# Attention, SoLU and a second network on one core: layer norm's transposes to the top of a block's first tile, the scores' softmax behind h's maximum, weight conversions up to the last tile

## The chip, the cores and the metric

The kernel runs on one core of a Trainium2 chip. The core has five engines that run side by side and wait for one another by semaphores: TensorE (PE: matrix multiplications; its weight loads are shown as PEld), VectorE (DVE), ScalarE (ACT), GpSimd (POOL) and SyncE (SP), which here issues nearly all transfers. Each engine works through its own queue in the order in which the program issues to it, so an instruction that waits holds up everything behind it on its engine. The metric is the time of one execution on the device in microseconds.

## What is computed

Batch 8, 8 heads, 576 positions, head size 64; 4608 tokens of width 512. Attention works in chunks of 64 positions. Its output passes through two networks:

```python
scores = 1/sqrt(64) * (q_chunk @ k_chunk.T);  attn = softmax(scores);  x = attn @ v_chunk
h  = x @ w_in                      # 512 -> 1024
solu = h * softmax(h)              # over the 1024
ln = (solu - mean) / sqrt(var + 1e-6) * g_ln
y  = ln @ w_out                    # 1024 -> 512
h2 = y @ w_in2                     # 512 -> 2048
out = leaky_relu(h2, 0.01) @ w_out2   # 2048 -> 512
```

The weights arrive as 64-bit floats and are converted on the core.

## The kernel before

**Precision.** Every large product is made of three: each operand is split into a high part (ScalarE copies it, rounding) and a low part (VectorE or GpSimd subtracts the high part), and high x high, high x low and low x high are summed.

**First half.** The tokens go through in 36 tiles of 128 (T = 36). A loop over t from 1 to 37 is a pipeline written out by hand: in round t, called tile t below, the program issues pieces of several tiles of tokens, and the order of the calls is the order on every engine.

- `qk_mm(t + 3)`, `softmax_a`, `softmax_b`, `pt_mm(t + 1)`, `pt_copy(t + 1)`, `pv_mm(t + 1)` are attention: the scores, their maximum and difference on VectorE and exponential on ScalarE (`softmax_a`), their sums on VectorE and the division on GpSimd (`softmax_b`), the transposes of the probabilities on TensorE (line 397, `pt_ps`), a copy to SBUF, and the product with v. `attend(t)` issues the product with v and the scores of a later tile into one pair of PSUM banks, and then `x_split` (lines 439, 444).
- `ff1_mm(t, 0)` and `ff1_mm(t, 1)` are the two halves of h (line 462, 12 matmuls each). h lives in three PSUM banks, so the second half of a tile's h takes the bank of the first half of the tile before.
- `solu_max` (line 477), `solu_a` (the minimum of two negated maxima, line 481; two exponentials on ScalarE, line 485), `solu_b` (the products on VectorE, line 493, which free h's banks), `solu_c` (sum of squares on ScalarE, line 513, and small factors on GpSimd) and `solu_d` (GpSimd scales the tile `us`, line 523) are SoLU and layer norm of tile t - 1.
- `lnT_mm(t - 2)` transposes the layer norm's result on TensorE (line 537), `lnT_hi` (ScalarE, line 548) and `lnT_lo` (VectorE, line 552) split it. These transposes and y share two PSUM banks.
- `y1_group(b, m)` is a quarter of y for a block b of four tiles (line 564, 24 matmuls); ScalarE copies it out (line 572) and SP stores it to `y_d`. Groups start in tile 5; from then on each tile has one. A tile with g = (t - 5) mod 4 = 0 is the first tile of a block of y: 5, 9, 13 to 33.

**Conversions.** The other weights come in pieces: `take_magnitudes` (ScalarE, line 103), `convert_a` and `convert_b` (four operations on VectorE, lines 110 to 120) and `finish`, which for two pieces together makes a weight block: two differences on GpSimd and two on VectorE (lines 193, 194), copies on ScalarE (196) and low parts on GpSimd (197). The block goes to DRAM by `store_next` in the next tile. The number `pieces` says how many pieces a tile converts: 1, or 2 in the tiles of the table DOUBLE. The first pieces are w_out1 (lines 126, 127, 173), which y needs from tile 5 on.

**Between the halves.** At t = 36 attention's memory is given back, and `y_load` (line 254) and `w_load` (line 294) fill the memory of the second half; `y_sum` (line 267) and `y_split` (lines 272, 273) make its operands at t = 37.

**Second half.** The second network by a scheme of seven products (lines 913, 970, 981) instead of eight. The change doesn't touch it.

Of the kernel before, what the change touches and what calls it, by code (L numbers as in the profile page):

```python
# [43 lines left out]
DOUBLE = (5, 6, 7, 14, 15, 22, 23, 30, 31)  # L44
# [8 lines left out]
def kernel(  # L53
# [254 lines left out]
    with tc.manual_schedule():  # L308

        with ExitStack() as phase:  # L310
# [271 lines left out]
            def attend(t):  # L582

                if AHEAD <= t < T - 3:
                    both = two_banks("xs_ps")
                    pv_mm(t + 1, both)
                    qk_mm(t + 3, both)
                    x_split(t + 1)
                    softmax_a(t + 3)
                else:  # L590
                    pv_mm(t + 1)
                    x_split(t + 1)
# [159 lines left out]
            for t in range(1, T + 2):  # L752
                if t == T:
                    att.close()
                    yp = ctx.enter_context(
                        tc.tile_pool(name="yp", bufs=1, side="right", reuse_waits="tile")
                    )
                    ws = ctx.enter_context(
                        tc.tile_pool(name="ws", bufs=WS, side="right", reuse_waits="tile")
                    )  # L760
                    for n in range(4):
                        y_load(0, n)
                    for _ in range(WS):
                        w_load()
# [13 lines left out]
                late = g == 0 or t == T - 1  # L778
                pieces = 0 if t < AHEAD or t >= T - 2 else 2 if t in DOUBLE else 1
# [4 lines left out]
                if 1 <= t <= T:  # L784
                    if t < 3:
                        solu_max(t - 1, 0)
                    solu_max(t - 1, 1)
                    solu_a(t - 1)
                if t <= AHEAD:
                    softmax_a(t + 2)  # L790
                if t > AHEAD and not late:
                    take_magnitudes(pieces)
                if 1 < t < T:
                    ff1_mm(t, 0)
                if 1 <= t <= T:
                    solu_b(t - 1)
# [4 lines left out]
                if t <= AHEAD or (late and t < T - 1):  # L801
                    pt_copy(t + 1)
                if late and t >= 2:
                    lnT_mm(t - 2)
                    lnT_split(t - 2, 0)
                    lnT_split(t - 2, 1)
                if t > AHEAD:
                    if late:
                        take_magnitudes(pieces)
                    convert_a(pieces)  # L810
                    convert_b(pieces)
                if AHEAD < t < T - 1 and not late:
# [8 lines left out]
                if 1 <= t <= T:  # L821
# [10 lines left out]
                if groups and not late:  # L832
# [4 lines left out]
                    if t >= 2:  # L837
                        lnT_mm(t - 2)
                        lnT_split(t - 2, 0)
                        lnT_split(t - 2, 1)  # L840
# [3 lines left out]
                else:  # L844
                    if t >= 2 and not late:
# [7 lines left out]
                    elif t < T - 1 and not late:  # L853
                        attend(t)
                    if 1 < t < T:
                        ff1_mm(t, 1)
                    if late and 1 < t < T - 1:
                        attend(t)
                    if t <= AHEAD:
                        if 2 <= t < AHEAD:  # L860
                            for hf in range(2):
                                lnT_lo(t - 2, hf)
                        finish()
                        take_magnitudes(pieces if t == AHEAD else t < 3)
                        convert_a(pieces if t == AHEAD else t == 3)
                        if t == AHEAD:
                            convert_b(pieces)
                    if t >= AHEAD:
                        finish(pieces)
                    for bm in groups:  # L870
                        y1_group(*bm)

# [295 lines left out]
```

## Time and profile before

| | |
|---|---|
| median of three runs | 1253.04 us (1252.58 to 1253.45) |
| the profiled execution: time, span | 1254.23 us, 1252.4 us |
| mean granted clock of TensorE, share of full speed | 0.993 |
| busy share: TensorE, its weight loads | 97%, 86% |
| busy share: VectorE, ScalarE, GpSimd | 71%, 46%, 23% |
| chain that ended last: TensorE, VectorE, ScalarE | 78%, 14%, 3% |

The span runs from the first to the last instruction; the time of an execution is some 2 us more. An engine's busy share is a mean over both halves: VectorE is busier in the first. The chain that ended last is followed back from the last instruction, at each step to what released it, so its shares say whose work or lateness stands in the time.

### The profile page before, as it was taken

The page shows a single profiled execution, that of the slowest core. Times are in us where ns is not written, and L with a number is a line of the kernel's source. Part 1 is how long each engine was busy: PE and PEld are TensorE (multiplying, and loading weights), DVE is VectorE, ACT ScalarE, POOL GpSimd, SP SyncE. Part 2 cuts the span into 40 slices and gives each one's busy share as a digit, 9 for nine tenths or more (in the row PEclk, how much of TensorE's full clock was granted, in tenths as well). Part 3 has the DMA queues.
Part 4 walks back from the last instruction along what each step waited for, and adds up shares of the span by engine and source line. Part 5 has one row for each costly group of instructions (what it writes and reads, how often), then busy time and mean ns, then how long its engine had stood idle before and what let it go on. Part 6 is the DMA issues. An engine that isn't in the chain of part 4 may idle for free.

```text
span 1252.4 us, 22880 instructions
## 1 busy us (share of the span) xinstructions
PE 1214.1 (97%) x8554; PEld 1074.5 (86%) x8554; DVE 895.5 (71%) x1536; ACT 573.1 (46%) x1079; POOL 284.1 (23%) x388
## 2 busy tenths in 40 slices
PE   4999999899999999999999999999999999999998
PEld 3777887787878777899889988998999899889987
DVE  7778878888887886535785677577666766775674
ACT  6655555555555554423443452344345333442451
POOL 0265656655765665100000000000000000000000
PEclk8899999999999999999999999999999999999999
DMA  7435456645756563469889878988998899789676
GB/s 249 142 111 175 153 184 211 237 160 168 239 184 194 191 194 130 143 214 316 270 284 318 281 242 274 324 256 253 297 307 246 261 303 298 240 264 296 195 224 197
DMA packets 153789, 288.83 MB, mean 231 GB/s; under 512 B 14288, under 2 KB 63440, under 8 KB 152656
## 3 DMA queue, kind: packets, MB, share of 16 engines
q1 hardware_dynamic: 153312, 286.78, 71.0%
q8 instruction: 69, 1.13, 0.4%
q10 hardware_dynamic: 368, 0.59, 0.1%
q14 instruction: 40, 0.33, 0.1%
HBM read 239.08 MB, written 48.23 MB: 229 GB/s over the span
## 4 chain that ended last, share of the span: by engine, by line
PE 78%; DVE 14%; ACT 3%; DMA 2%; issue 1%; POOL 1%; SPq 0%; ACTq 0%; POOLq 0%
PE h_ps L913 28%; PE o_ps L970 19%; PE y_ps L564 11%; PE o_ps L981 10%; PE h_ps L462 7%; DVE us L493 2%; DVE lnT L552 1%; DVE wf L116 1%; DVE wf L120 1%; DVE z L477 1%; DVE es L374 1%; DVE xs L444 1%; PE xs_ps L423 1%; DVE wf L110 1%; DVE st L373 1%
## 5 line engine op out<-in xcount | busy, mean ns | idle before, releaser
L913 PE MATMUL h_ps<-yo,w_s 128*128 128x384 f32 x2016 | 351.1, 335 | 0.0
L913 PEld LDWEIGHTS h_ps<-yo,w_s 128*128 128x128 f32 x2016 | 349.3, 188 | 0.7
L970 PE MATMUL o_ps<-wo_s,yo 128*128 128x512 f32 (+1 forms) x1016 | 262.9, 393 | 0.0
L462 PE MATMUL h_ps<-wi,xs 128*128 128x512 f32 x864 | 214.6, 402 | 12.0 <-DVE us L493 8.4
L564 PE MATMUL y_ps<-lnT,wo 128*128 128x512 f32 (+1 forms) x888 | 206.2, 388 | 4.6 <-DVE lnT L552 2.0
L970 PEld LDWEIGHTS o_ps<-wo_s,yo 128*128 128x128 f32 x1016 | 179.2, 188 | 28.6
L462 PEld LDWEIGHTS h_ps<-wi,xs 128*128 128x128 f32 x864 | 162.3, 192 | 48.0 <-DVE us L493 9.8
L564 PEld LDWEIGHTS y_ps<-lnT,wo 128*128 128x128 f32 x888 | 160.9, 188 | 38.8 <-POOL wo L127 3.2
L981 PEld LDWEIGHTS o_ps<-wo_s,yo 128*128 128x128 f32 x1008 | 144.7, 188 | 15.6
L273 DVE TENSOR_TENSOR yo<-c,yo 128x768 fp32r<-128x768 f32 x144 | 132.6, 954 | 31.9 <-ACT yo L272 31.9
L981 PE MATMUL o_ps<-wo_s,yo 128*128 128x256 f32 x1008 | 149.8, 283 | 0.0
L892 ACT ACTIVATE c<-h_c 128x384 f32<-128x384 f32 x144 | 72.8, 526 | 127.4 <-DVE h_c L924 127.4
L924 DVE TENSOR_TENSOR h_u<-h_ps,h_p 128x384 f32<-128x384 f32 x96 | 53.3, 555 | 106.7 <-PE h_ps L913 100.0
L272 ACT ACTIVATE yo<-c 128x768 fp32r<-128x768 f32 x144 | 113.0, 836 | 7.1 <-DVE c L954 5.5
L493 DVE SCALAR_TENSOR_TENSOR us<-h_ps,us 128x512 f32<-128x512 f32 x72 | 48.6, 691 | 32.7 <-ACT us L485 32.7
L552 DVE TENSOR_TENSOR lnT<-ln_ps,lnT 128x512 fp32r<-128x512 f32 x72 | 45.8, 680 | 33.8 <-ACT lnT L548 33.8
L387 POOL TENSOR_TENSOR es<-es,st 128x512 f32<-128x512 f32 x33 | 34.6, 1047 | 152.4 <-DVE st L386 96.8
L485 ACT ACTIVATE us<-h_ps,z 128x512 f32<-128x512 f32 x72 | 48.6, 681 | 34.3 <-DVE z L481 34.3
L272 ACT ACTIVATE yo<-a 128x768 fp32r<-128x768 f32 x36 | 29.9, 839 | 72.6 <-DVE a L267 72.6
L924 DVE TENSOR_TENSOR h_c<-h_ps,h_u 128x384 f32<-128x384 f32 x96 | 53.2, 554 | 12.8 <-PE h_ps L913 12.2
L380 ACT ACTIVATE es<-es 128x512 f32<-128x512 f32 x33 | 20.9, 632 | 86.7 <-DVE es L374 86.7
L892 ACT ACTIVATE c<-h_ps 128x384 f32<-128x384 f32 x48 | 23.6, 492 | 76.2 <-PE h_ps L913 76.2
(94 smaller groups left out, 1399.0 us busy)
## 6 DMA issues: line engine op xcount, KB each, us to landing
w_s<-wi_d SPq DMA_DIRECT2D x336, 256.0 KB, 4.0
wo_s<-wo_d SPq DMA_DIRECT2D x168, 512.0 KB, 4.6
wi_d<-wi SPq DMA_DIRECT2D x8, 1792.0 KB, 6.4
wo_d<-wi SPq DMA_DIRECT2D x8, 1792.0 KB, 7.2
raw<-in_w_out SPq DMA_DIRECT2D x24, 512.0 KB, 5.6
raw<-in_w_in SPq DMA_DIRECT2D x23, 512.0 KB, 5.3
vs<-in_v SPq DMA_DIRECT2D x144, 64.0 KB, 4.4
a<-y_d SPq DMA_DIRECT2D x24, 384.0 KB, 5.1
```

What stands on the lines that cost most here:

```text
L272: act.activation(o[:, 0], x, AF.Copy)
L273: dve.tensor_tensor(o[:, 1], x, o[:, 0].bitcast(F32), op=ALU.subtract)
L462: pe.matmul(hs[t, n], lhsT=x[:, a, kk, :], rhs=w[:, b, kk % 2, n, :], start=(kk == 0 and a == 0 and b == 0), stop=(kk == KD - 1 and a == 1),)
L485: act.activation(u[:, c], hs[t, n], AF.Exp, bias=z[:, 0:1], accum_out=z[:, 8 + n : 9 + n])
L493: dve.scalar_tensor_tensor(u[:, c], hs.pop((t, n)), 1.0 / FF1, u[:, c], op0=ALU.mult, op1=ALU.mult, accum_out=z[:, 10 + n : 11 + n],)
L552: dve.tensor_tensor(dst[:, 1], ps, dst[:, 0].bitcast(F32), op=ALU.subtract)
L564: pe.matmul(ps[:, part], lhsT=w[:, a, kk % 4, m * P : (m + 1) * P], rhs=lnT[:, c, kk, pairs, :][:, part], start=(kk == 0 and a == 0 and c ...
L892: act.activation(blocks[block, j // 2][:, j % 2], src, AF.Prelu, alpha=0.01)
L913: pe.matmul(ps, lhsT=w[:, a, kk * P : (kk + 1) * P], rhs=y[:, c, kk, :], start=(first and kk == 0 and a == 0 and c == 0), stop=(kk == 1 an ...
L924: dve.tensor_tensor(o, ps, x, op=ALU.add)
L970: pe.matmul(ps[:, : 2 * P * (a.stop - a.start)], lhsT=x[:, 0, kk, m * P : (m + 1) * P], rhs=w[:, kk, a].rearrange("p a n -> p (a n)"), sta ...
L981: pe.matmul(sums[p % 2][m][:, : 2 * P], lhsT=x[:, 1, kk, m * P : (m + 1) * P], rhs=w[:, kk, 0], start=False, stop=(i == PAIRS - 1 and kk = ...
```

## The change

Four things move; no arithmetic is added or removed.

1. In a block's first tile from 9 on (`late`), layer norm's transposes and their high parts go to the top of the tile, ahead of h's maximum, and y's group goes from the end of the tile to the middle, ahead of `attend`. Tile 35 is no longer such a tile.
2. `softmax_a` leaves `attend`. It comes at the top of the next tile, behind h's maximum and `solu_a`.
3. DOUBLE loses 30 and 31, and single conversions go on in tiles 34 and 35 instead. The last store is issued at t = 36 ahead of the loads of y.
4. Tile 5's two conversions start behind the probabilities' copy and end ahead of `solu_c`, not behind `attend`.

The diff, cut to these:

```diff
-DOUBLE = (5, 6, 7, 14, 15, 22, 23, 30, 31)
+DOUBLE = (5, 6, 7, 14, 15, 22, 23)
...
                     both = two_banks("xs_ps")
                     pv_mm(t + 1, both)
                     qk_mm(t + 3, both)
-                    x_split(t + 1)
-                    softmax_a(t + 3)
                 else:
                     pv_mm(t + 1)
-                    x_split(t + 1)
+                x_split(t + 1)
...
                 if t == T:
+                    store_next()
                     att.close()
...
-                late = g == 0 or t == T - 1
-                pieces = 0 if t < AHEAD or t >= T - 2 else 2 if t in DOUBLE else 1
+                late = g == 0 and t > AHEAD
+                pieces = 0 if t < AHEAD or t >= T else 2 if t in DOUBLE else 1
...
-                if 1 <= t <= T:
+                if late:
+                    lnT_mm(t - 2)
+                    for hf in range(2):
+                        lnT_hi(t - 2, hf)
+                if t <= T:
                     if t < 3:
                         solu_max(t - 1, 0)
                     solu_max(t - 1, 1)
                     solu_a(t - 1)
-                if t <= AHEAD:
+                if late:
+                    for hf in range(2):
+                        lnT_lo(t - 2, hf)
+                if t + 2 < T:
                     softmax_a(t + 2)
-                if t > AHEAD and not late:
+                if t > AHEAD:
                     take_magnitudes(pieces)
...
-                if t <= AHEAD or (late and t < T - 1):
+                if t <= AHEAD:
                     pt_copy(t + 1)
-                if late and t >= 2:
+                if t == AHEAD:
+                    take_magnitudes(pieces)
                     lnT_mm(t - 2)
-                    lnT_split(t - 2, 0)
-                    lnT_split(t - 2, 1)
+                    for hf in range(2):
+                        lnT_split(t - 2, hf)
                 if t > AHEAD:
-                    if late:
-                        take_magnitudes(pieces)
                     convert_a(pieces)
                     convert_b(pieces)
-                if AHEAD < t < T - 1 and not late:
+                if AHEAD < t < T - 1:
                     pt_copy(t + 1)
...
+                elif t == AHEAD:
+                    convert_a(pieces)
+                    convert_b(pieces)
...
-                if groups and not late:
+                if t > AHEAD and groups:
                     for bm in groups:
                         y1_group(*bm)
                     if t + 1 < T:
                         attend(t)
-                    if t >= 2:
+                    if not late:
                         lnT_mm(t - 2)
-                        lnT_split(t - 2, 0)
-                        lnT_split(t - 2, 1)
+                        for hf in range(2):
+                            lnT_split(t - 2, hf)
                     if t < T:
                         ff1_mm(t, 1)
                     finish(pieces)
```

TensorE at tile 9, the first tile of a block of y, from the end of tile 8 on. Before (`ln_ps` are layer norm's transposes, four rows of `h_ps` are half an h, `pt_ps` the probabilities' transposes, `y_ps` a group of y):

```order
L462 MATMUL h_ps<-wi_172,xs 128x512 x2
L462 MATMUL h_ps<-wi_353,xs 128x512 x2
L397 MATMUL pt_ps<-ident,es 128x128 x4
L537 MATMUL ln_ps<-ident,us 128x128 x8
L462 MATMUL h_ps<-wi_172,xs 128x512 x4
L462 MATMUL h_ps<-wi_353,xs 128x512 x4
L462 MATMUL h_ps<-wi_172,xs 128x512 x2
L462 MATMUL h_ps<-wi_353,xs 128x512 x2
L423 MATMUL xs_ps<-pt,vs_104 64x64 x16
L360 MATMUL xs_ps<-kb_102,qt 64x64 x16
L564 MATMUL y_ps<-lnT,wo_831 128x512 x12
L564 MATMUL y_ps<-lnT,wo_960 128x512 x12
```

The same place after:

```order
L537 MATMUL ln_ps<-ident,us 128x128 x8
L462 MATMUL h_ps<-wi_172,xs 128x512 x4
L462 MATMUL h_ps<-wi_353,xs 128x512 x4
L462 MATMUL h_ps<-wi_172,xs 128x512 x2
L462 MATMUL h_ps<-wi_353,xs 128x512 x2
L397 MATMUL pt_ps<-ident,es 128x128 x4
L564 MATMUL y_ps<-lnT,wo_831 128x512 x12
L564 MATMUL y_ps<-lnT,wo_960 128x512 x12
L423 MATMUL xs_ps<-pt,vs_104 64x64 x16
L360 MATMUL xs_ps<-kb_102,qt 64x64 x16
L462 MATMUL h_ps<-wi_172,xs 128x512 x4
```

Layer norm's transposes went ahead of the first half of h, and y's group stands between the halves of h instead of behind the second.

VectorE from the end of tile 11 into tile 12, an ordinary tile. Before (L373 and L374 are the scores' maximum and difference, L552 layer norm's low parts, L193 and L194 a weight block, L477 h's maximum, L493 the products, L384 the scores' sums):

```order
L444 TENSOR_TENSOR xs<-xs_ps,xs 128x2x2x128
L373 TENSOR_REDUCE st_2766<-xs_ps 128x8
L374 TENSOR_TENSOR es<-xs_ps,st_2766 128x512
L552 TENSOR_TENSOR lnT<-ln_ps,lnT 128x4x128 x2
L193 TENSOR_TENSOR wc<-wf,wc 128x256
L194 TENSOR_TENSOR wc<-wf,wc 128x256
L477 TENSOR_REDUCE z<-h_ps 128x1
L481 TENSOR_TENSOR z<-z 128x1
L493 SCALAR_TENSOR_TENSOR us,z<-h_ps,us 128x512 x2
L502 TENSOR_TENSOR z<-z 128x1
L384 TENSOR_REDUCE st_2766<-es 128x8
```

The same place after:

```order
L444 TENSOR_TENSOR xs<-xs_ps,xs 128x2x2x128
L552 TENSOR_TENSOR lnT<-ln_ps,lnT 128x4x128 x2
L193 TENSOR_TENSOR wc<-wf,wc 128x256
L194 TENSOR_TENSOR wc<-wf,wc 128x256
L477 TENSOR_REDUCE z<-h_ps 128x1
L481 TENSOR_TENSOR z<-z 128x1
L373 TENSOR_REDUCE st_2818<-xs_ps 128x8
L374 TENSOR_TENSOR es<-xs_ps,st_2818 128x512
L493 SCALAR_TENSOR_TENSOR us,z<-h_ps,us 128x512 x2
L502 TENSOR_TENSOR z<-z 128x1
L384 TENSOR_REDUCE st_2818<-es 128x8
```

The scores' maximum and difference went from ahead of layer norm's low parts to between h's maximum and the products.

SP where the halves meet, before (`wo_d` is a weight block's store, `a` the four loads of y: a11, a21, a22, a12; in brackets what a transfer waits for):

```order
L135 DMA wo_d_84<-wi 896x1x512 [waits DMAHW7_49,Pool_49]
L577 DMA y_d_72<-ys 128x256 [waits DMAHW0_49,Activation_49]
L580 DMA y_d_71<-ys 128x256 [waits DMAHW1_49]
L254 DMA a_5911<-y_d_67 128x2x384 [waits DMAHW2_49,DVE_49]
L254 DMA a_5913<-y_d_67 128x2x384 [waits DMAHW3_49]
L254 DMA a_5915<-y_d_67 128x2x384 [waits DMAHW7_49,DMAHW4_49]
```

And after:

```order
L135 DMA wo_d_84<-wi 896x1x512 [waits DMAHW6_49,Pool_49]
L577 DMA y_d_72<-ys 128x256 [waits DMAHW7_49,Activation_49]
L580 DMA y_d_71<-ys 128x256 [waits DMAHW0_49]
L135 DMA wo_d_84<-wi 896x1x512 [waits DMAHW1_49,Pool_49]
L254 DMA a_5911<-y_d_67 128x2x384 [waits DMAHW2_49,DVE_49]
L254 DMA a_5913<-y_d_67 128x2x384 [waits DMAHW3_49]
L254 DMA a_5915<-y_d_67 128x2x384 [waits DMAHW6_49,DMAHW4_49,DMAHW1_49]
```

A second store stands ahead of the loads of y; it waits for GpSimd, and the third load (a22) waits for it to land (DMAHW1).

## Rows read from the trace of the kernel before

**Rows 1.** Timeline of TensorE: start us, length us, line, operation, count [idle before, releaser].

```profile
90.53 0.60 PE L397 MATMUL pt_ps<-ident,es 128*128 128x128 f32 x4
...
93.46 5.29 PE L564 MATMUL y_ps<-lnT,wo 128*128 128x512 f32 x22 [0.83 <-POOL wo L127]
...
134.82 0.60 PE L397 MATMUL pt_ps<-ident,es 128*128 128x128 f32 x4
...
175.47 0.60 PE L397 MATMUL pt_ps<-ident,es 128*128 128x128 f32 x4
...
188.98 0.60 PE L397 MATMUL pt_ps<-ident,es 128*128 128x128 f32 x4
...
191.59 3.02 PE L462 MATMUL h_ps<-wi,xs 128*128 128x512 f32 x12 [1.13 <-DVE us L493]
...
203.97 0.60 PE L397 MATMUL pt_ps<-ident,es 128*128 128x128 f32 x4
...
231.01 0.60 PE L397 MATMUL pt_ps<-ident,es 128*128 128x128 f32 x4
232.23 5.73 PE L564 MATMUL y_ps<-lnT,wo 128*128 128x512 f32 x24 [0.62 <-DVE lnT L552]
...
246.48 0.60 PE L397 MATMUL pt_ps<-ident,es 128*128 128x128 f32 x4
...
262.38 0.60 PE L397 MATMUL pt_ps<-ident,es 128*128 128x128 f32 x4
...
477.88 4.61 PE L462 MATMUL h_ps<-wi,xs 128*128 128x512 f32 x12 [1.68 <-DVE us L493]
...
508.07 11.08 PE L564 MATMUL y_ps<-lnT,wo 128*128 128x512 f32 x48
```

**Rows 2.** One window, TensorE: us, busy us (count), granted clock, DMA share, GB/s.

```profile
479.00:480.00 1.00, 1.00 (x4) 0.50 0.02 8
```

**Rows 3.** Timeline of VectorE, end of tile 11 and tile 12.

```profile
170.42 0.68 DVE L373 TENSOR_REDUCE st<-xs_ps 128x8 f32<-128x512 f32 x1
...
173.07 1.29 DVE L552 TENSOR_TENSOR lnT<-ln_ps,lnT 128x512 fp32r<-128x512 f32 x2 [1.24 <-ACT lnT L548]
174.28 1.42 DVE L193 TENSOR_TENSOR wc<-wf,wc 128x256 f32<-128x256 f32 x1
...
176.49 0.68 DVE L477 TENSOR_REDUCE z<-h_ps 128x1 f32<-128x512 f32 x1
...
178.42 0.69 DVE L493 SCALAR_TENSOR_TENSOR us<-h_ps,us 128x512 f32<-128x512 f32 x1 [1.06 <-ACT us L485]
...
181.60 1.15 DVE L112 TENSOR_SCALAR wf<-wf 128x512 uint32<-128x512 uint32 x1
```

**Rows 4.** Timeline of GpSimd: the scaling of `us` in tiles 12 and 16.

```profile
185.60 1.21 POOL L523 TENSOR_SCALAR us<-us,z 128x1024 f32<-128x1024 f32 x1
...
244.00 1.20 POOL L523 TENSOR_SCALAR us<-us,z 128x1024 f32<-128x1024 f32 x1
```

**Rows 5.** Timeline of VectorE, one conversion in tile 13 and what follows it.

```profile
194.51 0.43 DVE L110 TENSOR_SCALAR wf<-wf 128x512 f32<-128x512 f32 x1
194.97 0.43 DVE L112 TENSOR_SCALAR wf<-wf 128x512 uint32<-128x512 uint32 x1
...
196.80 0.68 DVE L477 TENSOR_REDUCE z<-h_ps 128x1 f32<-128x512 f32 x1
```

**Rows 6.** Timeline of VectorE where the halves meet.

```profile
505.69 1.29 DVE L552 TENSOR_TENSOR lnT<-ln_ps,lnT 128x512 fp32r<-128x512 f32 x2 [0.49 <-ACT lnT L548]
...
523.57 0.95 DVE L267 TENSOR_TENSOR s<-a,a 128x768 f32<-128x768 f32 x1
```

**Rows 7.** DMA issues from 480 to 560 us: count, KB each, median us to landing.

```profile
wo_d<-wi SPq DMA_DIRECT2D x1, 1792.0 KB, 7.1
a<-y_d SPq DMA_DIRECT2D x4, 384.0 KB, 5.2
```

**Rows 8.** Timeline of ScalarE where the halves meet.

```profile
532.63 0.60 ACT L572 ACTIVATE ys<-y_ps 128x512 f32<-128x512 f32 x1 [1.08 <-issue]
```

More of the change, by code (lines that the diff above doesn't have):

```diff
@@ L794 @@
                     ff1_mm(t, 0)
-                if 1 <= t <= T:
+                if t <= T:
                     solu_b(t - 1)
@@ L820 @@
                     owed = 1
-                if 1 <= t <= T:
+                elif t == AHEAD:
+                    convert_a(pieces)
+                    convert_b(pieces)
+                if t <= T:
                     solu_c(t - 1)
@@ L844 @@
                 else:
-                    if t >= 2 and not late:
+                    if t >= 2 and t != AHEAD:
                         lnT_mm(t - 2)
@@ L852 @@
                         ff1_mm(t, 1, (3,))
-                    elif t < T - 1 and not late:
+                    elif t < AHEAD:
                         attend(t)
-                    if 1 < t < T:
+                    if 1 < t:
                         ff1_mm(t, 1)
-                    if late and 1 < t < T - 1:
+                    if t == AHEAD:
                         attend(t)
[L859 to L869, printed above, removed]
+                    if 2 <= t < AHEAD:
+                        for hf in range(2):
+                            lnT_lo(t - 2, hf)
+                    finish()
+                    if t < 3:
+                        take_magnitudes()
+                    elif t == 3:
+                        convert_a()
                     for bm in groups:
```

## The prediction

> **What bounds the kernel now.** I read the page's busy shares first (in the table above: TensorE 97%, VectorE 71%), then TensorE's own timeline, because an engine that is busy for 97% of the span can only give back its gaps. In the second half (matrix multiplications of the second network, from 543 us on) there are none to speak of, and the change does not touch that half; so I looked for gaps between 75 and 543 us. The timeline shows a beat: each tile issues its four transposes of probabilities once, and from one such row to the next an undisturbed tile takes 13.51 us, from 175.47 to 188.98 [rows 1]. Whatever a tile takes above that is loss. The reader should see five kinds:
>
> - Tiles 6 to 8: 90.53 to 134.82 is 44.29 us for three tiles, 3.76 too many; part of it is y's first group, which waits for w_out1 pieces that GpSimd is still splitting (0.83 in one place).
> - Tile 13, first of a block of y: 14.99, so 1.48 too many. Its second half of h waits 1.13 for VectorE to read the previous h out of PSUM (191.59). Tiles 21 and 29 repeat it with 1.50 and 1.47.
> - Tile 16, after two tiles of double conversions: 15.47, 1.96 too many; y waits for layer norm's low parts on VectorE (232.23). Tiles 24 and 32 repeat it (1.95, 1.96).
> - Tile 17, first of a block and just behind: 15.90, 2.39 too many; tile 25 repeats it (2.38).
> - Tile 33: the same wait (1.68), and then its 12 matmuls take 4.61 where those of tile 13 took 3.02 [rows 1]; the granted clock there is 0.50, the 1.2 GHz level [rows 2]. TensorE had been nearly idle before the drop; the like waits of tiles 17 and 25 had none. I put the loss at 2.39 + 1.59 = 3.98.
>
> Sum: 3.76 + 4.45 + 5.87 + 4.77 + 3.98 = 22.8 us. That is all that the touched part could give.
>
> **The change, part by part.** *Transposes first, y in the middle.* In a block's first tile before, y came last, since layer norm's transposes of that very tile had to come ahead of it; so between the first half of h and the second only short work stood (two groups of transposes), while VectorE needed maximum, exponential and product. Now y's group, with probabilities and scores, stands there as in every other tile, some 7 us more. The waits on h of tiles 13, 21, 29, 17, 25 and 33 go: before, the product in tile 12 ended near 179.8, 7 us behind the end of the previous h [rows 3], and the second half of h comes 13.51 less its own 2.75, so 10.8, behind it. No instruction is added; TensorE issues the same ones.
>
> What can be late instead is the transposes: they now stand at the tile's top, and read u, which GpSimd scales in the tile before. In tile 12 of before, that scaling ends at 185.60 + 1.21 = 186.81 [rows 4], while TensorE would want it at about 188.98 less some 2.75 for 12 matmuls, 186.2 [rows 1]. As things stood, 0.6 late; so what the second edit does to that chain decides.
>
> *Scores' softmax behind h's maximum.* Before, VectorE made the scores' maximum and difference ahead of layer norm's low parts: from 170.42 to 171.83, then it sat idle for 1.24 because ScalarE's high parts stood behind the scores' exponential, which stood behind that difference [rows 3]. Only then came the low parts, a weight block's two differences (174.28 to 176.49) and h's maximum at 176.49, though h had been finished around 172.7. Moved behind the maximum, 1.41 of work and 1.24 of idling leave this stretch: maximum 2.65 earlier. The work falls where VectorE waits 1.06 for h's exponentials anyway, at 178.42 [rows 3], so it costs 0.35 there and not 1.41. Net 2.3 earlier for all that follows, the scaling too: ready at about 184.5 for 186.2. I take no wait in tiles 9, 13, 21, 29 and 33. Scores' exponentials come later by about 5 us, but their transposes come a tile later, so that is covered.
>
> In double tiles VectorE has 2.3 us more of conversions (one takes 194.51 to 196.80 [rows 5]), and its lag adds up: in tile 16 of before the scaling ended at 245.20 [rows 4], and TensorE without its waits would have wanted it at about 246.48 - 2.75 - 1.4 = 242.3. It has to come 2.9 earlier. Two double tiles in a row win 2 x 2.3 = 4.6, or less, since part of the idling was lag that the conversions fill. I take no wait in tiles 17 and 25, with bounds of 0 and 2 each, and count 0.4 for the pair. Tiles 16, 24 and 32 lose their wait on the low parts, now 2.65 earlier against 0.62 of wait [rows 1]; in tile 32 the double conversions ahead are gone too.
>
> *Tile 5's conversions* start behind h's maximum instead of behind the attention's work, some 4 us earlier. They then delay the next x's low part, by 4.6 for two; its user comes after y's first group, which takes 5.5 (half of 11.08 for two at 508.07 [rows 1]), so about 1 is to spare. In return tile 6's weights are split earlier, but GpSimd's multiplication by g now stands ahead of layer norm's factors, so only about 1 us earlier. I take 1.0 off tile 6's loss and all 1.6 off tiles 7 and 8, since everything behind has slack: 2.8 of 3.76, bounds 0 and 3.76.
>
> One rule was weighed here. VectorE's shift of a piece took 0.43 in tile 13 and 1.15 in tile 12 [rows 3, 5]; in tile 12 GpSimd multiplied the probabilities at that moment. The Trainium skill, SBUF — State Buffer, section "Who interferes with whom", says that VectorE's two-port forms and GpSimd hold a shared pair of ports alternately, one blocking the other for a whole instruction. By that rule tile 5's conversions, moved under GpSimd's scaling, would lose up to two such 0.7, 1.4 in all, and the sum would be 0.4 smaller past the cover of 1; the trace agrees with the rule. My sum goes without it.
>
> *Conversions up to the last tile.* Two pieces move from tiles 30 and 31 to 34 and 35. In tile 35 one conversion (2.3 us) and h's maximum (0.68) now precede layer norm's low parts, which ran at 505.69 [rows 6] with y starting at 508.07 [rows 1]. VectorE can begin at about 505.1, so the first low part ends at about 508.8 and y waits 0.8: I take 0.9, bounds 0 and 2. Behind it the last weight block is made in tile 36: GpSimd ends it at about 515.5, and SP now issues its store ahead of the loads of y. The third load (a22) waits until that store has landed, since it takes its memory: 7.1 later, then 5.2 for itself [rows 7], so about 528 where the sum that needs it began at 523.57 [rows 6]. The chain of sums and splits ends 4.5 us later, and with it ScalarE's copy of y's second group, 532.63 before with 1.08 of idling [rows 8], about 536.6 then. Its bank is wanted by y's fourth group at about 538.5. Hidden, with 2 us left; were the block 4 us later, it would cost 2.
>
> **Sum.** Gains 2.8 + 4.45 + 5.87 + 4.77 + 3.98 = 21.9; costs 0.9 + 0.4 = 1.3; net -20.6. The profiled execution took 1254.23, 1.19 over the median of the runs, 1253.04; taken off the median this gives **1232.5 us**, and about 1233.6 for a profiled run.
>
> **The rivals.** (1) *The double tiles stay late.* GpSimd's scaling is too late at the top of tiles 17 and 25 by 2 each, and tiles 16 and 24 keep their 1.96: 7.9 lost, about 1240. For it: VectorE is loaded nearly in full there. The Trainium skill, TensorE: Matmul & The Clock Gate, section "What's actually happening", says that an idle array falls back to 1.2 GHz; tile 33 agrees, tiles 17 and 25 do not. If such a wait brings the slow level as in tile 33, 1.6 more, 1242. Chance 17%.
> (2) *The transposes wait in all seven block tops*, because the softmax in front of the product delays the scaling and nothing else gives the time back: 0.6 + 1.4 = 2.0 each, 14 in all, 1246.5. Against it: the 1.24 of idling has one cause, and that leaves. Chance 6%.
> (3) *The end of the stage*: the store is later than I reckon, and y's last group and the first product wait 3 to 6: 1236 to 1239. Chance 10%.
> (4) *Slower than before*: the same wait as in (2), but more than 20.6 / 7 = 2.9 us each, that is, the scaling 2.3 later than in the rows instead of 2.3 earlier; at 4 us each it would be 1260. The exponentials now stand behind layer norm's high parts on ScalarE in these tiles, 1.1 us; that alone is not enough. Chance 3%. No change to within 0.2% (2.5 us, about what a measurement of this kernel can tell from none) would need 18 us of new waits: 2%.
>
> My forecast has the remaining 62%, with 1230 to 1235 of its own. All 22.8 without any cost would be 1230.2; rival (1) ends at 1240. The range 1229.5 to 1240.5 leaves out rival (1) with the slow clock, (2) and (4). Faster 95%, same 2%, slower 3%.
>
> **What the profile of after would show.** Transposes of probabilities 13.5 us apart from tile 9 to 32; no wait of h on u's product in the tiles named; the granted clock at full through tile 33; h's maximum within 1.5 us of the end of h in ordinary tiles; a wait of about 0.9 of y near the end of the first half; the load of a22 landing some 5 us before y's fourth group. Wrong would be: transposes of layer norm that wait for u on GpSimd, or y's last groups waiting for ScalarE's copies.

## The result, and the profile after

The changed kernel took **1233.01 us** (median of 5 runs, 1231.88 to 1233.18) against 1253.24 (5 runs) for the kernel before on the same chip: ratio 0.984, 95% interval [0.982, 0.985]. The prediction was 1232.5. The total is right; what it put the gain down to is not, as the runs below show.

The page of after: TensorE's share rises from 97% to 98% of a shorter span, and VectorE now waits for TensorE where TensorE waited for VectorE. Columns of the last two rows: line, engine, operation, form, count, then busy us, mean ns, and idle us with its releaser.

```profile
span 1230.9 us, 22882 instructions
...
PE 1208.2 (98%) x8554; PEld 1073.7 (87%) x8554; DVE 900.8 (73%) x1536; ACT 573.1 (47%) x1079; POOL 285.9 (23%) x388
...
L477 DVE TENSOR_REDUCE z<-h_ps 128x1 f32<-128x512 f32 x72 | 48.9, 682 | 20.6 <-PE h_ps L462 20.6
...
L552 DVE TENSOR_TENSOR lnT<-ln_ps,lnT 128x512 fp32r<-128x512 f32 x72 | 46.0, 681 | 6.5 <-ACT lnT L548 6.5
```

The page of before has of the same kind:

```profile
L493 DVE SCALAR_TENSOR_TENSOR us<-h_ps,us 128x512 f32<-128x512 f32 x72 | 48.6, 691 | 32.7 <-ACT us L485 32.7
L552 DVE TENSOR_TENSOR lnT<-ln_ps,lnT 128x512 fp32r<-128x512 f32 x72 | 45.8, 680 | 33.8 <-ACT lnT L548 33.8
```

The low parts (line 552) idled 33.8 us for ScalarE's high parts, 8.2 of them in one wait near the end of the first half; now 6.5, 4.8 of them in one wait. That row holds the cause, as will be seen, but its size alone doesn't tell: the products (line 493) idled nearly as long.

TensorE's timeline at tiles 13, 17 and 33 and at the end of the first half, which answers to [rows 1]:

```profile
182.63 1.03 PE L537 MATMUL ln_ps<-ident,us 128*128 128x128 f32 x8
183.42 3.02 PE L462 MATMUL h_ps<-wi,xs 128*128 128x512 f32 x12
186.27 0.60 PE L397 MATMUL pt_ps<-ident,es 128*128 128x128 f32 x4
...
236.77 1.03 PE L537 MATMUL ln_ps<-ident,us 128*128 128x128 f32 x8
...
453.33 1.03 PE L537 MATMUL ln_ps<-ident,us 128*128 128x128 f32 x8
454.12 3.02 PE L462 MATMUL h_ps<-wi,xs 128*128 128x512 f32 x12
...
486.48 11.18 PE L564 MATMUL y_ps<-lnT,wo 128*128 128x512 f32 x48 [0.47 <-DVE lnT L552]
497.50 1.91 PE L537 MATMUL ln_ps<-ident,us 128*128 128x128 f32 x16
499.57 22.38 PE L564 MATMUL y_ps<-lnT,wo 128*128 128x256 f32 x120 [0.15 <-DVE lnT L552]
521.78 3.47 PE L915 MATMUL h_ps<-yo,w_s 128*128 128x384 f32 x19
```

No wait is left at the tops of blocks, and the 12 matmuls behind tile 33's transposes take 3.02; those that waited there before took 4.61. The granted clock is 1.00 from 130 to 520 us, the 2.4 GHz level. The second half starts at 521.78; before, at 543.26. The transposes of probabilities are 13.5 us apart in ordinary tiles, as forecast; at block tops they now stand behind layer norm's, so a tile of 14.43 and one of 12.66 follow each other there. Neither sign of being wrong is seen: no transpose waits for GpSimd, and y's last groups don't wait for copies.

VectorE in tile 12 answers to [rows 3]:

```profile
166.79 1.28 DVE L552 TENSOR_TENSOR lnT<-ln_ps,lnT 128x512 fp32r<-128x512 f32 x2
167.99 1.37 DVE L193 TENSOR_TENSOR wc<-wf,wc 128x256 f32<-128x256 f32 x1
169.39 0.84 DVE L194 TENSOR_TENSOR wc<-wf,wc 128x256 f32<-128x256 f32 x1
170.16 0.68 DVE L477 TENSOR_REDUCE z<-h_ps 128x1 f32<-128x512 f32 x1
...
172.28 0.68 DVE L493 SCALAR_TENSOR_TENSOR us<-h_ps,us 128x512 f32<-128x512 f32 x1
```

Both idle times of [rows 3], 1.24 and 1.06, are gone. h's maximum starts some 1.1 behind the end of h (near 169.1); before, 3.8. GpSimd's scaling answers to [rows 4]; in tile 16:

```profile
234.94 1.20 POOL L523 TENSOR_SCALAR us<-us,z 128x1024 f32<-128x1024 f32 x1
```

It ends at 236.14, 0.63 ahead of the transposes at 236.77; in tile 12 the margin is 2.16 (180.47 to 182.63).

Where the halves meet, y's copies by ScalarE answer to [rows 8]:

```profile
513.61 1.18 ACT L572 ACTIVATE ys<-y_ps 128x512 f32<-128x512 f32 x2 [1.02 <-DMA y_d<-ys]
```

The second of the two starts at about 514.2 (513.61 + 1.18 - 0.60), 27.7 behind y's start at 486.48, against 24.6 before (532.63 - 508.07); the prediction had 28.5 and called it hidden, as it is: the y that runs from 499.57 has no gap, and its fourth group, which wants that bank, begins near 516.5. The sum that needs a22 begins at 505.10, when that load lands, some 11 us ahead of the fourth group; the 5 that the prediction names among its signs doesn't fit its own sum (528 and 538.5).

### The profile page after: what moved, and what is told of

It reads as the page before. It is cut to its first block, busy times and chain, and to the rows that moved or that the text cites. A ratio compares the mean times of both kernels' runs of the same rounds, so it can differ in the third digit from the quotient of the medians.

```text
span 1230.9 us, 22882 instructions
## 1 busy us (share of the span) xinstructions
PE 1208.2 (98%) x8554; PEld 1073.7 (87%) x8554; DVE 900.8 (73%) x1536; ACT 573.1 (47%) x1079; POOL 285.9 (23%) x388
## 3 DMA queue, kind: packets, MB, share of 16 engines
q8 instruction: 69, 1.13, 0.4%
## 4 chain that ended last, share of the span: by engine, by line
PE 93%; DVE 5%; ACT 1%; POOL 1%; issue 0%; DMA 0%; POOLq 0%; ACTq 0%
PE h_ps L915 28%; PE o_ps L972 19%; PE y_ps L564 16%; PE h_ps L462 14%; PE o_ps L983 10%; PE ln_ps L537 2%; PE xs_ps L423 1%; PE pt_ps L397 1%; PE xs_ps L360 1%; DVE wf L116 1%; DVE wf L120 1%; DVE z L477 1%; DVE us L493 1%; DMA raw<-in_w_in 0%; DVE wf L110 0%
## 5 line engine op out<-in xcount | busy, mean ns | idle before, releaser
L972 PEld LDWEIGHTS o_ps<-wo_s,yo 128*128 128x128 f32 x1016 | 179.3, 189 | 28.5
L477 DVE TENSOR_REDUCE z<-h_ps 128x1 f32<-128x512 f32 x72 | 48.9, 682 | 20.6 <-PE h_ps L462 20.6
L572 ACT ACTIVATE ys<-y_ps 128x512 f32<-128x512 f32 x36 | 21.5, 597 | 82.8 <-PE y_ps L564 81.7
L552 DVE TENSOR_TENSOR lnT<-ln_ps,lnT 128x512 fp32r<-128x512 f32 x72 | 46.0, 681 | 6.5 <-ACT lnT L548 6.5
```

The lines of the kernel that those rows point to most:

```text
L477: dve.reduce_max(sol[t][:, 8 + n : 9 + n], hs[t, n], axis=AX, negate=True)
L552: dve.tensor_tensor(dst[:, 1], ps, dst[:, 0].bitcast(F32), op=ALU.subtract)
L972: pe.matmul(ps[:, : 2 * P * (a.stop - a.start)], lhsT=x[:, 0, kk, m * P : (m + 1) * P], rhs=w[:, kk, a].rearrange("p a n -> p (a n)"), sta ...
```

## The experiments

Each median below stands beside runs of the kernel before on the same chip: 1252.35 for the first four runs, 1253.08 for the next four, 1252.02 for the next three, 1253.98 for the last. "The edits" are numbered as under "The change". The theory at the start was the prediction's: edit 1 is worth 13.2 us (tiles 13, 17, 21, 25, 29, 33), edit 2 5.9 (tiles 16, 24, 32), edit 4 2.8, edit 3 about nothing. The rival: the block tops waited because VectorE was late, so edit 2 is worth nearly all.

**All but edit 2.** After, with the softmax back in `attend`:

```diff
                     qk_mm(t + 3, both)
+                    x_split(t + 1)
+                    softmax_a(t + 3)
...
-                if t + 2 < T:
+                if t <= AHEAD:
                     softmax_a(t + 2)
```

> The kernel after, with the scores' softmax back in attend, ahead of layer norm's low parts. Mine: the first edit alone moves waits to the transposes at the tops, because GpSimd's scaling comes too late: about 0.6 us each in tiles 13, 21, 29 and 33, 1 to 3 in tiles 17 and 25, and tiles 16 and 24 keep their 1.96; together 8 to 12, so 1241 to 1245, and the trace names u on GpSimd as the releaser of the transposes. Rival (the edits simply add; the softmax only helps the double tiles): 1237, no wait of a transpose on GpSimd.

Measured: **1266.3** us, ratio 1.011 [1.009, 1.013]: slower than before, which neither my theory nor the rival had. TensorE at the top of tile 13, and three windows, one in its wait and two behind it (us, busy us of PE, PEld, DVE, ACT, POOL with counts, granted clock, DMA share, GB/s):

```profile
181.61 3.01 PE L462 MATMUL h_ps<-wi,xs 128*128 128x512 f32 x12
186.94 1.23 PE L537 MATMUL ln_ps<-ident,us 128*128 128x128 f32 x8 [2.32 <-DVE lnT L552]
187.86 4.61 PE L462 MATMUL h_ps<-wi,xs 128*128 128x512 f32 x12
```

```profile
185.00:186.00 1.00, 0.00 (x0) 0.00 (x0) 0.00 (x0) 1.00 (x3) 0.01 (x1) 1.00 0.99 301
...
188.00:189.00 1.00, 1.00 (x4) 0.81 (x4) 0.92 (x3) 0.99 (x3) 0.00 (x0) 0.50 0.73 243
189.00:190.00 1.00, 1.00 (x4) 0.81 (x3) 1.00 (x2) 1.00 (x4) 0.00 (x0) 0.50 0.57 154
```

The releaser is not GpSimd's scaling, which the prediction watched (it ended at 185.01), but VectorE's low parts of the transposes before: these must be read out of their banks before the next transposes can be written there. All seven block tops wait so, 16.7 us in all (0.95, four times 2.3, twice 3.2), and behind six of them the clock falls to 1.2 GHz. ScalarE and VectorE there:

```profile
184.96 0.63 ACT L380 ACTIVATE es<-es 128x512 f32<-128x512 f32 x1 [3.46 <-DVE es L374]
185.50 1.07 ACT L548 ACTIVATE lnT<-ln_ps 128x512 fp32r<-128x512 f32 x2
```

```profile
184.23 0.69 DVE L374 TENSOR_TENSOR es<-xs_ps,st 128x512 f32<-128x512 f32 x1
186.11 1.29 DVE L552 TENSOR_TENSOR lnT<-ln_ps,lnT 128x512 fp32r<-128x512 f32 x2 [1.18 <-ACT lnT L548]
```

Difference on VectorE, exponential on ScalarE, high parts on ScalarE, low parts on VectorE: four steps one behind the other. That is the row to keep in mind for the last four runs.

**Edit 2 alone.** The kernel before, with `softmax_a` moved as in after and nothing else:

```diff
-                    softmax_a(t + 3)
...
-                if t <= AHEAD:
+                if t + 2 < T:
                     softmax_a(t + 2)
```

> The kernel before, with nothing but the scores' softmax moved behind h's maximum. Mine: tiles 16, 24 and 32 lose their 1.96 each and tiles 17 and 25 some 0.4 each, but in the block tops 13, 17, 21, 25, 29 and 33 the wait of h grows by about 0.5, because the softmax (1.4) stands ahead of the products and only 0.85 of idling takes it up: about 4 us faster than before, 1249, with h's wait at tile 13 grown from 1.13 to about 1.7. Rival (the softmax costs nothing where it stands): 1246.5, h's wait at tile 13 unchanged or gone.

Measured: **1232.3**, ratio 0.984 [0.982, 0.985], as much as all four edits. From 75 us to the second half TensorE waits once, for 0.15; from tile 8 to 32 no tile is over 0.1 longer than 13.52. In tile 13, where y still comes last, VectorE waits for h and TensorE's second half of h follows the transposes at once:

```profile
183.00 0.69 DVE L477 TENSOR_REDUCE z<-h_ps 128x1 f32<-128x512 f32 x1 [1.24 <-PE h_ps L462]
...
185.74 0.69 DVE L493 SCALAR_TENSOR_TENSOR us<-h_ps,us 128x512 f32<-128x512 f32 x1
```

```profile
185.97 1.04 PE L537 MATMUL ln_ps<-ident,us 128*128 128x128 f32 x8
186.76 3.01 PE L462 MATMUL h_ps<-wi,xs 128*128 128x512 f32 x12
```

So the short work between the halves suffices: it was VectorE that came late, not TensorE that had too little to do.

**All but edit 1**: after, with the transposes, y and `attend` of a block's first tile in the places of before.

```diff
-                if late:
+                if t > T:
                     lnT_mm(t - 2)
                     for hf in range(2):
...
+                if late and t < T:
+                    lnT_mm(t - 2)
+                    for hf in range(2):
+                        lnT_split(t - 2, hf)
+                    take_magnitudes(pieces)
...
+                if late and t < T:
+                    ff1_mm(t, 1)
+                    attend(t)
+                    finish(pieces)
+                    for bm in groups:
+                        y1_group(*bm)
```

> The kernel after, with the block tops 9 to 33 as before (layer norm's transposes behind the probabilities', y last); the other edits stay. Mine: h waits for its products in all of tiles 13 to 33 that are block tops, some 2 each, so 10 to 13 slower than after, 1244 to 1246; whether the clock falls to 1.2 GHz at tile 33 is open, and 1.6 hang on it. Rival (the softmax's move alone gives most): within 5 of after, below 1238.

Measured: **1232.4**, ratio 0.984 [0.982, 0.985]. No wait at any block top, the clock full: the prediction's theory is gone.

**All but edit 4**: tile 5's conversions behind `attend` again.

```diff
                 if t == AHEAD:
-                    take_magnitudes(pieces)
...
-                elif t == AHEAD:
-                    convert_a(pieces)
-                    convert_b(pieces)
...
+                    elif t == AHEAD:
+                        take_magnitudes(pieces)
+                        convert_a(pieces)
+                        convert_b(pieces)
+                        finish(pieces)
```

> The kernel after, with tile 5's two conversions back behind the attention's work. Mine: tiles 6 to 8 lose about 2.8 again, 1235.8; y waits for w_out1's low parts on GpSimd in each of the three. Rival (the softmax's move has already taken this loss away): 1233, and only tile 6 waits.

Measured: **1231.8**, ratio 0.983 [0.982, 0.985]; the rival was right that the softmax's move had taken this loss away. Tiles 6 to 8 take 41.74 us together where those of after take 42.09: without edit 4 they are 0.35 shorter, not longer, and the wait of tile 6 for GpSimd's w_out1 pieces is gone.

**All but edit 3**: DOUBLE with 30 and 31, no conversions in tiles 34 and 35, the last store as before.

```diff
-DOUBLE = (5, 6, 7, 14, 15, 22, 23)
+DOUBLE = (5, 6, 7, 14, 15, 22, 23, 30, 31)
...
-                    store_next()
...
-                pieces = 0 if t < AHEAD or t >= T else 2 if t in DOUBLE else 1
+                pieces = 0 if t < AHEAD or t >= T - 2 else 2 if t in DOUBLE else 1
```

> The kernel after, with the conversions as before: tiles 30 and 31 double, none in 34 and 35, the last store in tile 34. Mine: the third edit is worth nothing by itself. The wait of y at tile 36 (0.47) goes, and tile 33's transposes come as close to the scaling as those of tiles 17 and 25 (0.6 of margin): 1232.5, within 0.5 of after. Rival (the third edit took tile 32's loss away and kept tile 33 from the slow clock): 1235 or more, with a wait at tile 32 or 33.

Measured: **1231.8**, ratio 0.983 [0.981, 0.984]. The wait of 0.47 at y's last groups is gone, and tiles 32 and 33 have none: edit 3 brings nothing on top of edit 2.

**How much room the scaling has.** GpSimd scales `us` once more (by 1, the result is the same) ahead of each block top; in the second run three times more.

```diff
+                if 7 <= t <= 31 and t % 4 == 3:
+                    for _ in range(1):
+                        pool.tensor_scalar(u, u, 0.0, 1.0, op0=ALU.add, op1=ALU.mult)
```

> The kernel after, with GpSimd scaling u once more, by 1, for the tiles that the block tops 9 to 33 transpose (seven more operations of 1.2 us, the result the same). Mine: the margins at the tops are 2.2 in tiles 13, 21, 29, 33 and 0.6 in tiles 17 and 25, so only these two wait, 0.6 each: 1234.2. Rival (the transposes' place has no slack, or the extra work delays the conversions as well): seven times 1.2, 1241.

> The same with three more scalings, 3.6 us each time. Mine: 3.6 less 3.0 in tile 9, less 2.2 in tiles 13, 21, 29 and 33, less 0.6 in tiles 17 and 25: 0.6 + 5.6 + 6.0 = 12.2, so 1245, and the transposes wait for GpSimd in all seven. Rival (high parts, exponentials and products behind the transposes pass the delay on, so that h waits as well, or the clock falls): 1250 or more.

Measured: **1233.3** with one, ratio 0.985 [0.983, 0.986], and **1245.5** with three, 0.994 [0.992, 0.995]. With one, tiles 17 and 25 alone wait, by 0.45 and 0.44. With three all seven wait, 10.5 in all; the three take 3.4 us together, not 3.6. Tile 17 with three (line 526 is the added scaling, line 540 is 537 of after):

```profile
240.60 1.09 PE L540 MATMUL ln_ps<-ident,us 128*128 128x128 f32 x8 [2.70 <-POOL us L526]
241.45 3.02 PE L462 MATMUL h_ps<-wi,xs 128*128 128x512 f32 x12
```

So the margins of 0.63 and 2.16 are real, and the chain through GpSimd, on which rivals (1), (2) and (4) were built, is the right second chain, only not the one that ends last.

**The wait of y's last groups.** After, with tile 35's transposes ahead of its conversion:

```diff
+                if t == T - 1:
+                    lnT_mm(t - 2)
+                    for hf in range(2):
+                        lnT_split(t - 2, hf)
                 if t > AHEAD:
                     convert_a(pieces)
...
-                    if t >= 2 and t != AHEAD:
+                    if t >= 2 and t != AHEAD and t != T - 1:
                         lnT_mm(t - 2)
```

> The kernel after, with tile 35's layer norm transposes and their parts issued ahead of its conversion. Mine: the wait of y at tile 36 (0.47) goes and nothing takes its place, 1232.5, which is inside the noise of the time; the profile tells. Rival (the conversion then delays the last weight block, so that y's last groups wait for ScalarE): 1233 to 1234, with a wait of y's fourth group on ScalarE's copy.

Measured: **1232.4**, ratio 0.984 [0.982, 0.985]. The 0.47 is gone, but the last transposes now wait 0.85 for the scaling (499.64): a wait exchanged for another.

**Which part of edit 2.** The prediction gave it two sizes: 1.41 of VectorE's work that leaves the stretch ahead of h's maximum, and 1.24 of idling on ScalarE. The kernel before, with ScalarE's exponential alone moved behind h's exponentials; VectorE's order is that of before throughout (its lines from 373 on are numbered 4 to 6 higher):

```diff
             def softmax_a(t):
+                softmax_dve(t)
+                softmax_exp(t)
+
+            def softmax_dve(t):
...
-                act.activation(e, e, AF.Exp, scale=scale)
+
+            def softmax_exp(t):
+                act.activation(es[t], es[t], AF.Exp, scale=scale)
...
-                    softmax_a(t + 3)
+                    softmax_dve(t + 3)
...
                 if t <= AHEAD:
                     softmax_a(t + 2)
+                elif t + 2 < T:
+                    softmax_exp(t + 2)
```

> Kernel before, with only ScalarE's exponential of the scores moved (into the next tile, behind h's exponentials); VectorE's maximum and difference of the scores stay where they were, ahead of the low parts. My theory now: VectorE's lag behind TensorE is made of two pieces, 1.41 us of scores' work and 1.24 us of idling on ScalarE's high parts; this run takes away the second alone. h's maximum in tile 12 comes about 1.2 earlier (near 175.3). Waits of 1.13 vanish, those of 1.68 shrink to about 0.4, y's wait in tiles 16, 24 and 32 vanishes: about 1236, 1233 to 1239. Rival: the order on VectorE is what counts, and the idling only moves to another wait: 1249 to 1253. Second rival: ScalarE's order is the whole of it: 1232 with no wait left.

Measured: **1232.6**, ratio 0.985 [0.983, 0.986]. One instruction of ScalarE per tile, moved, gives the whole gain to within the intervals; the second rival was right in the time. No wait for VectorE is left from tile 6 on but the 0.15 at y's last groups; y still waits 0.32 and 0.40 for GpSimd's w_out1 pieces in tiles 6 and 7. ScalarE in tile 12 of before, where the cost was:

```profile
171.92 0.63 ACT L380 ACTIVATE es<-es 128x512 f32<-128x512 f32 x1 [2.14 <-DVE es L374]
172.46 1.07 ACT L548 ACTIVATE lnT<-ln_ps 128x512 fp32r<-128x512 f32 x2
```

and VectorE of this run:

```profile
167.77 0.69 DVE L378 TENSOR_TENSOR es<-xs_ps,st 128x512 f32<-128x512 f32 x1
168.38 1.28 DVE L558 TENSOR_TENSOR lnT<-ln_ps,lnT 128x512 fp32r<-128x512 f32 x2
169.57 0.76 DVE L193 TENSOR_TENSOR wc<-wf,wc 128x256 f32<-128x256 f32 x1
170.36 0.43 DVE L194 TENSOR_TENSOR wc<-wf,wc 128x256 f32<-128x256 f32 x1
170.71 0.68 DVE L483 TENSOR_REDUCE z<-h_ps 128x1 f32<-128x512 f32 x1
```

The low parts follow the difference at once. The tile stands 3.37 earlier than in before (ScalarE's copy of x at 165.81, not 169.18), so the maximum, 170.71 against 176.49, is 2.4 earlier within its tile: 1.24 of idling, and 1.1 because the weight block's two differences take 1.14 together and not 2.21 (176.49 - 174.28 in [rows 3]).

**Edit 1 alone**, in the kernel before (edits 2 to 4 not made; the lines of edit 1 as under "The change"):

```diff
-                late = g == 0 or t == T - 1
+                late = g == 0 and t > AHEAD
...
+                if late:
+                    lnT_mm(t - 2)
+                    for hf in range(2):
+                        lnT_hi(t - 2, hf)
```

> Kernel before with the first edit alone: transposes of layer norm at the top of a block's first tile, y between the halves of h; softmax, conversions of tile 5 and of the last tiles as before. My theory now: the first edit without the second trades the wait of h for a longer one of the transposes on VectorE's low parts, and the clock falls behind most of these waits: 1264 to 1270 (the run without the second edit took 1266.3). Rival: the prediction's step, by which y between the halves of h is worth 13 us: 1240 to 1244. Second rival: the loss in the run without the second edit came from edits three and four together with it: 1250 to 1256.

Measured: **1273.0**, ratio 1.017 [1.015, 1.018]: 21 us slower, in direction as I then expected, 3 more than my range. The seven tops wait 17.6 us for low parts. Tile 13:

```profile
189.74 1.16 PE L537 MATMUL ln_ps<-ident,us 128*128 128x128 f32 x8 [2.31 <-DVE lnT L552]
190.66 4.58 PE L462 MATMUL h_ps<-wi,xs 128*128 128x512 f32 x12
```

The 6.8 us over the run with edits 3 and 4 besides stand nearly all in tiles 6 to 8 (3.0 more) and tile 32 (3.6 more): without edit 2, edits 4 and 3 do what they were counted for.

**The exponential alone, with edits 1, 3 and 4**: after, with VectorE's part of the softmax back ahead of the low parts.

```diff
                     qk_mm(t + 3, both)
+                    x_split(t + 1)
+                    softmax_dve(t + 3)
...
-                if t + 2 < T:
+                if t <= AHEAD:
                     softmax_a(t + 2)
+                elif t + 2 < T:
+                    softmax_exp(t + 2)
```

> Changed kernel, in which VectorE's maximum and difference of the scores go back to the attention's place ahead of the low parts, and only ScalarE's exponential stays behind h's. Against the run with the whole softmax back, whose transposes at the block tops waited 0.95, four times 2.3 and twice 3.2 for low parts, this takes 1.24 of idling away. My theory: waits of about 1.1 four times and 2.0 twice, 8 us in all, 1240 to 1242 as long as the clock stays full; with the clock at half behind the two longer ones up to 1245. Rival: VectorE's order decides alone, so 1260 to 1268. Second rival: ScalarE's order alone, no wait left, 1232 to 1234.

Measured: **1235.2**, ratio 0.986 [0.985, 0.988]. Two waits are there that after doesn't have, of 1.03 and 1.06 at the tops of tiles 17 and 25:

```profile
238.32 1.17 PE L543 MATMUL ln_ps<-ident,us 128*128 128x128 f32 x8 [1.03 <-DVE lnT L558]
```

So with the transposes at the top VectorE's 1.41 does count, by some 2.7 us (15.76 and 15.78 in these tiles, 14.43 each in after); ScalarE's order counts for 31 (1266.3 to 1235.2). My sum for this run, 8 us of waits, took 1.24 off each wait of the first run; more than that went, and how much of it is lag carried over from tile to tile was not tried.

**Two neighbours change places.** The kernel before, in which ScalarE does layer norm's high parts first and the exponential behind them, in the same tile; a block's first tile is left as it was:

```diff
-                    softmax_a(t + 3)
+                    softmax_dve(t + 3)
+                    if t % 4 == 1:
+                        softmax_exp(t + 3)
...
                     lnT_split(t - 2, 1)
+                    if t < T - 3:
+                        softmax_exp(t + 3)
```

> Kernel before, in which ScalarE's two neighbouring steps change places in every tile but a block's first: layer norm's high parts first, the scores' exponential behind them, still in the same tile; nothing else moves on any engine. My theory now: the exponential ahead of the high parts, which itself waits for VectorE's difference, is the whole of the loss, since VectorE's low parts wait for those high parts: no wait of TensorE left at tiles 12 to 33, 1232 to 1234. Rival: the exponential has to leave the stretch between attention and h's maximum altogether, since ScalarE then comes to the weights' high parts and h's exponentials 0.6 late: 1236 to 1241. Second rival: nothing changes, since the exponential's place in the next tile was what counted: 1249 to 1253.

Measured: **1234.6**, ratio 0.985 [0.983, 0.986], the same ratio as with the exponential moved away. From tile 8 to 32 no tile is over 0.1 longer than 13.52; tile 6 keeps its 2.1, behind tile 5, which as a block's first was left as it was. ScalarE and VectorE in tile 12:

```profile
168.55 1.08 ACT L554 ACTIVATE lnT<-ln_ps 128x512 fp32r<-128x512 f32 x2
170.73 0.63 ACT L386 ACTIVATE es<-es 128x512 f32<-128x512 f32 x1 [1.10 <-DVE es L378]
```

```profile
169.95 0.69 DVE L378 TENSOR_TENSOR es<-xs_ps,st 128x512 f32<-128x512 f32 x1
170.56 1.28 DVE L558 TENSOR_TENSOR lnT<-ln_ps,lnT 128x512 fp32r<-128x512 f32 x2
...
173.52 0.68 DVE L483 TENSOR_REDUCE z<-h_ps 128x1 f32<-128x512 f32 x1
```

The exponential still waits (1.10 here), but the high parts no longer stand behind it.

No version tried is faster than after by more than the runs spread: TensorE is busy for 98% of the span in all that come near it.

## Why the prediction was right, and where it was wrong

**The total** follows from the first step, which held: TensorE can give back its gaps and no more, these were 22.8 us, and nearly all went. From the transposes of tile 5 (76.93 before, 76.44 now) to the second half (543.26, 521.78) 21.0 are gained, where 20.6 were forecast. Of the costs, y's wait near the end was 0.47 for a forecast of 0.9, and the 0.4 at tiles 17 and 25 didn't come; 0.35 of y's wait for GpSimd's w_out1 pieces is left in tile 6 (0.83 in [rows 1]); with edit 2 and without edit 4 it isn't there. The boundary stayed hidden, as predicted.

**"Transposes first, y in the middle" is the step that failed.** It put 13.2 us to edit 1: "between the first half of h and the second only short work stood". True of the order, but not the cause. Alone that edit costs 21 us, as the transposes at the top wait 17.6 for VectorE's low parts; the prediction let them wait for GpSimd's scaling only and left the banks that they write out of its sum. Taken out of after, the edit changes nothing. The wait of 1.13 in [rows 1] named VectorE, whose maximum stood at 176.49 for an h that had ended near 172.7 [rows 3]: 3.8 of lag, of which 1.13 was too much. Both numbers were in the prediction, for edit 2, and were not set against the wait that it gave to edit 1. Had they been, some 1.7 off the lag would have seemed enough for the longest of these waits (1.68). Within tile 12, counted from ScalarE's copy of x, the maximum comes 1.8 earlier with the swap, 2.4 with the exponential alone and 2.7 with the whole edit (predicted 2.65), and none of the three has a wait left at a block top.

**"Scores' softmax behind h's maximum" was right in mechanism and short in size**: 5.87 predicted for tiles 16, 24 and 32, 20.0 measured with edit 2 alone. Within it the 1.24 of idling was the part that counted, and the 1.41 of VectorE's work is worth nothing in the order of before and some 2.7 us once edit 1 is there. No run takes the 1.24 away by itself: with it the weight block's two differences got shorter, by 1.1 with the exponential alone and by 0.4 with the swap. The prediction named ScalarE's order as the cause of the idling; it didn't follow the row to the page's total of 33.8 us. Beside it the products' 32.7 on the page is as large and was no cause: it is 35.0 in the run with the exponential alone.

**"Tile 5's conversions"** (2.8) and **the double tiles of edit 3** exist without edit 2 (3.0 and 3.6 in the run with edit 1 alone against that with 1, 3 and 4), and are paid twice with it: each repairs lag that edit 2 has already taken away. Gains that remove the same lag don't add up; the prediction added them, and the sum came out right since it was bounded by the gaps and not by the edits. That the edits together would close all gaps was in part luck: for the change without edit 2, adding gave 1237, and 1266.3 was measured.

**The rivals.** (2) and (4) had the right place, the block tops, and the wrong releaser: without edit 2 the transposes wait 0.95 to 3.2 for low parts on VectorE, not for the scaling. (1) was near: 0.63 of margin in tiles 17 and 25. (3) did not happen.

## What to carry to other kernels

Where one engine's step waits for a second engine and a third step behind it feeds the second engine back, look at the order of the two on the engine between: a step that waits must not stand ahead of one that is ready. Before costing an edit by the work it moves, set each wait of the busiest engine beside the lag of the engine that it names, and take the lag's own cause first: here all waits on VectorE that came of one lag went with it, and the other cures for them added nothing. Moving a consumer earlier when its producer is late can only shift the wait, here onto banks that the late engine had still to read.

## What the runs showed of the hardware that was not expected

**The clock does not follow the length of the wait alone.** After idle times of 2.3 and 3.2 us at block tops (edits 1, 3 and 4) it fell to 1.2 GHz, in some of them during the transposes, and the 12 matmuls behind took 3.75 to 5.00 in place of 3.02. After 2.70 and 2.76 at the tops of tiles 17 and 25 (scaling three times more), where edits 1, 3 and 4 had waited 3.2 behind the same work, it stayed at 2.4 GHz. In before, 1.68 brought it down in tile 33 [rows 1] and 1.68 in tile 17 did not:

```profile
249.99 3.02 PE L462 MATMUL h_ps<-wi,xs 128*128 128x512 f32 x12 [1.68 <-DVE us L493]
```

Each is one profiled execution; over other executions of the scaling run the mean clock was 0.993 to 0.997. What decides between these was not settled; a forecast of a wait there has to carry both.

**VectorE's work on SBUF data takes longer beside GpSimd's.** VectorE's 128x256 difference (line 193) took 1.37 in tile 12 of after, within two subtractions of GpSimd (line 197) that ran from 167.79 to 169.95; the same form (line 194) took 0.43 in the run with the exponential alone, begun at 170.36, after GpSimd had ended at 170.05. GpSimd in after, then in the run with the exponential alone:

```profile
167.79 2.16 POOL L197 TENSOR_TENSOR wi<-wf,wi 128x512 fp32r<-128x512 f32 x2 [0.37 <-ACT wi L196]
```

```profile
168.05 2.00 POOL L197 TENSOR_TENSOR wi<-wf,wi 128x512 fp32r<-128x512 f32 x2 [0.70 <-ACT wi L196]
```

The Trainium skill, SBUF — State Buffer, section "Who interferes with whom", has the two share a pair of ports; these rows agree. The price moves with the order: it was 1.1 of the 2.4 by which moving the exponential brought the maximum forward in tile 12.
